# The order in which a ring of streamed weight tiles is filled, and when the last weights and weight sums are prepared, in a fused attention and two-MLP kernel

## The chip, the cores and the metric

One core of one Trainium2 chip runs the whole program. The metric is the device time of one execution in microseconds (us). TensorE (PE) does the matrix products and accumulates in PSUM; VectorE (DVE), ScalarE (ACT) and GpSimd (POOL) do the elementwise work; SyncE (SP) issues the transfers, each in program order: a transfer that waits holds back all that stands behind it in SP's queue.

## The reference

Attention in both directions between a sequence (512 rows) and a state (32 rows) for 8 batches and 8 heads, and then two MLPs on the 8 x 544 = 4352 rows that come out of it:

```python
x = np.ascontiguousarray(attn_out.transpose(0, 2, 1, 3)).reshape(B * S, H * D)

def _moe_ref(x, w_gate, w_val, w_out):      # d_model 512, d_ff 1536
    g = x @ w_gate
    silu = g * (1.0 / (1.0 + np.exp(-g)))
    return silu * (x @ w_val) @ w_out

def _moe2_ref(x, w_in, w_out):              # d_model 512, d_ff 2048
    h = x @ w_in
    g = h * (1.0 / (1.0 + np.exp(-1.702 * h)))
    return g @ w_out
```

All of the change lies in and around the second MLP, `_moe2_ref`.

## The kernel before, in words

Every fp32 operand of a product is kept as two tiles, a high part (a cast to `F32R`) and a low part (what the cast left over); a product is three matmuls: high by high, low by high, high by low. So each operand costs a cast on ACT and a subtraction on DVE (for activations, the helper `cut`, lines 720 to 722) or on POOL (for weights, lines 235 and 236).

Stage 1 (attention and the first MLP) runs block by block over the rows, and writes its result `y1` to DRAM. During its last block the weights of the second MLP are read and cut, in the order i2 0, o2 0, i2 1, o2 1, ... (`i2 f` is the f-th slice of `w_in`, `o2 f` that of `w_out`, F2 = 16 slices each). `need(key)` drives this: it runs `w_step` until that weight's cut has been recorded, and each step also asks for a later weight's transfer. At the end of stage 1 the slices up to 13 are done; i2 14, o2 14, i2 15 and o2 15 are not. The cut `o2` slices are also stored to DRAM as `w2b`, since their tiles in SBUF are wanted for other things.

Stage 2 (the loop at the end) goes over nine row blocks `n`: n = 0 is the block of the 256 state rows, n = 1 to 8 are the eight sequence blocks of 512 rows.

- n = 0 and n = 1: for each f, `mm_in` computes the hidden slice f (12 matmuls into one of the two `gv` buffers of PSUM), ACT takes a sigmoid, DVE multiplies (L1164), `to_h` cuts the result into a tile `h` and puts it into the list `waiting`. When more than two are waiting, `out2` takes the oldest and multiplies it with `o2 f` into the accumulators `acc0` to `acc3` (L330 to L332, three matmuls for each accumulator).
- n = 2 to 8: `four(n, p)` computes two hidden slices, 2p and 2p+1, at once, by Strassen's scheme: seven half-size products (42 matmuls of 256 columns, L1104 to L1106) of sums of weights with sums of activations. At its end it puts slice 2p+1 into `waiting` first and slice 2p second:

```python
        to_h(n, 2 * p + 1, sg, S)
        v.tensor_tensor(sf, one, sf, op=ALU.mult)
        to_h(n, 2 * p, sf, S)
```

  The two `out2` calls inside the next `four` consume them in that order. In the text such a `four` with its two `out2` is a pair.

From n = 1 on the `o2` slices no longer lie in SBUF; they are streamed back from `w2b` through a ring of three tiles `wo`. The list `stream2` says which slice is loaded next; `next_out` takes the next entry, puts it into ring place `s % 3` and issues one transfer of 512 KB on SP (L934). It is called three times at n = 0, f = 8, and then once at the end of each `out2`. A load into a ring place waits, on SP, until TensorE has used the tile that lies there.

The sums of weights that `four` needs are made during n = 0 and n = 1, for each of the PAIRS = 8 pairs of `i2` slices: `mix_load(p)` reads two `i2` slices back into a tile `sr` (two transfers, L960), `mix(p)` makes three sums on POOL (L974 to L976, in place in `sr`), casts them on ACT into tiles `wc` (L982) and takes the low parts on POOL (L983); `mix_store` writes full `wc` chunks to DRAM (`w2c`), from where `next_chunk` streams them again through another ring of three (L944) in n = 2 to 8. One more difference for each pair is made late, in n = 1 and just before n = 2 (`mix_late`, L989 to L992), from half slices (L958), and replaces a part of `i2`. `mix_step(n, f)` decides which of these run after step f: in the kernel before, a load in one step and all of `mix` in the next.

The other names that the rows use: `xr` are rows of `y1` read for the next block (L788, L1023), `xo` their cut parts, `ev` the copies of the accumulators on the way out (`evac`, L732 and L733), `sg` and `wt` working tiles.

Of the kernel before, what the change touches and what calls it, by code (L numbers as in the profile page):

```python
# [12 lines left out]
ALU = mybir.AluOpType  # L13
# [60 lines left out]
def kernel(  # L74
# [33 lines left out]
    F2 = FF2 // P  # L108
# [6 lines left out]
    v, a, pe, pool_e, sy = nc.vector, nc.scalar, nc.tensor, nc.gpsimd, nc.sync  # L115
# [19 lines left out]
    def f32(t):  # L135
        return t.bitcast(F32)
# [155 lines left out]
    def w_step(lead=2):  # L292
        w_join()
        if pos["begun"] > pos["done"]:
            w_end()
        w_dma()
        while pos["begun"] < len(stream):
            if pos["begun"] >= pos["done"] + (lead if stream[pos["begun"]][2] else 1):
                break
            w_begin()  # L300
            w_dma()

    def need(key):
        while pos["done"] <= where[key]:
            w_step()


    def mm_in(ps, w, xop, N, ks=range(KD)):

        for k in ks:  # L310
            xh, xl = xop[k]
            wh, wl = w[:, 0, k * P : (k + 1) * P], w[:, 1, k * P : (k + 1) * P]
            pe.matmul(ps[:, :N], wh, xh, start=k == 0, stop=False)  # L313
            pe.matmul(ps[:, :N], wl, xh, start=False, stop=False)  # L314
            pe.matmul(ps[:, :N], wh, xl, start=False, stop=k == KD - 1)  # L315
# [21 lines left out]
    def gv():  # L337
        return psg.tile([P, 512], F32, name="gv", tag="gv")
# [443 lines left out]
    def x2_step(n, f, at_f):  # L782

        N = NT if order2[n] == B else S
        for k in range(KD):
            if f == at_f + 2 * k:
                x2raw[k] = x2p.tile([P, 512], F32, name="xr", tag="xr", bufs=1)
                sy.dma_start(x2raw[k][:, :N], y1[order2[n]][k // 2][:, k % 2, :])  # L788
            if f == at_f + 2 * k + 2:
                xs2.setdefault(n, {})[k] = x_tiles(xp if n % 2 else x2q, k, N)  # L790
                cut(*xs2[n][k], x2raw.pop(k)[:, :N])

    order2 = [B] + list(range(B))
# [121 lines left out]
    Q = S // 2  # L915
    PAIRS = F2 // 2
# [5 lines left out]
    def slot(f, shape, name, dt=F32R):  # L922
        pl, tag = slot2[f]
        return pl.tile(shape, dt, name=name, tag=tag, bufs=1)

    stream2 = [(n, f) for n in range(1, len(order2)) for f in range(F2)]
    outs = {(0, f): units["o2", f] for f in range(F2) if ("o2", f) in units}
    pos2 = {"outs": 0, "chunks": 0}

    def next_out():  # L930
        s = pos2["outs"]
        if s < len(stream2):
            outs[stream2[s]] = t = slot(s % 3, [P, 2, DM], "wo")
            sy.dma_start(f32(t), both2[stream2[s][1]])  # L934
            pos2["outs"] += 1
# [3 lines left out]
    def next_chunk(load=True):  # L939
        c = pos2["chunks"]  # L940
        if c < NCH * (len(order2) - 1):
            mixed[c] = t = slot(3 + c % 3, [P, 2, 2, Q], "wc")
            if load:
                sy.dma_start(f32(t), chunks[c % NCH])  # L944
            pos2["chunks"] += 1

    def mixed_at(n, i):

        i += 3 * PAIRS * (n - 1)
        return mixed[i // 2][:, i % 2]  # L950

    sraw = {}

    def mix_load(p, late=False):
        sraw[p] = r = work.tile([P, 2, DM], F32, name="sr", tag="raw", bufs=RAWS)
        for j in range(2):
            if late:
                sy.dma_start(r[:, j, :Q], whole2["i2", 2 * p + j][:, :Q])  # L958
            else:
                sy.dma_start(r[:, j, :], whole2["i2", 2 * p + j])  # L960
# [3 lines left out]
    def mix_store():  # L964
        while full:
            c = full.pop(0)
            sy.dma_start(chunks[c], f32(mixed[c]))

    def mix(p):

        r = sraw.pop(p)
        a11, a12, a21, a22 = (r[:, j, c * Q : c * Q + Q] for j in range(2) for c in range(2))
        t = pool_e.tensor_tensor
        t(a22, a21, a22, op=ALU.add)  # L974
        t(a11, a22, a11, op=ALU.subtract)
        t(a12, a12, a11, op=ALU.subtract)  # L976
        for i, src in enumerate((a11, a22, a12)):
            k = 3 * p + i
            if k % 2 == 0:
                next_chunk(False)  # L980
            to = mixed_at(1, k)
            a.copy(to[:, 0], src)  # L982
            t(to[:, 1], src, f32(to[:, 0]), op=ALU.subtract)  # L983
            if k % 2 == 1:
                full.append(k // 2)

    def mix_late(p):
        r = sraw.pop(p)
        pool_e.tensor_tensor(r[:, 1, :Q], r[:, 0, :Q], r[:, 1, :Q], op=ALU.subtract)  # L989
        to = units["i2", 2 * p + 1][:, :, :Q]  # L990
        a.copy(to[:, 0], r[:, 1, :Q])
        pool_e.tensor_tensor(to[:, 1], r[:, 1, :Q], f32(to[:, 0]), op=ALU.subtract)  # L992

    def mix_step(n, f):

        mix_store()
        if n == 0 and f >= 7:
            if f % 2:
                mix_load((f - 7) // 2)
            else:  # L1000
                mix((f - 8) // 2)
        elif n == 1:
            if f in (0, 2, 4, 6):
                mix(4 + f // 2)
            if f in (1, 3, 5):
                mix_load(5 + f // 2)
            if f == 8:
                for _ in range(3):
                    next_chunk()
            if f >= 8:  # L1010
                if f > 8:
                    mix_late(f - 9)
                mix_load(f - 8, True)

    xs3 = {}
    xraw = {}
# [1 line left out]
    def x3_step(n, f):  # L1018

        if f == 1:  # L1020
            for j in range(2):
                xraw[j] = r = slot(XRAW[j], [P, 2, S], "xr", F32)
                sy.dma_start(r, y1[order2[n]][j])  # L1023
        if f < 3:
            return
        b11, b12 = xraw[0][:, :, :Q], xraw[0][:, :, Q:]
        b21, b22 = xraw[1][:, :, :Q], xraw[1][:, :, Q:]
        ops = {
            3: (0, b11),
            4: (b11, b12, b11),  # L1030
            5: (2, b22),
            6: (b12, b22, b12),
            7: (4, b11),
            8: (b11, b22, b11),
            9: (5, b11),
            10: (1, b21),
            11: (b21, b11, b21),
            12: (6, b12),
            13: (3, b21),
        }  # L1040
        op = ops.get(f)
        if op is None:
            return
        if len(op) == 3:
            v.tensor_tensor(op[0], op[1], op[2], op=ALU.subtract)
            return
        k, src = op
        if k < 4:
            t = (xp if n % 2 else x2q).tile([P, 2, 2, Q], F32R, name="xo", tag=f"x{k}")
        else:  # L1050
            t = slot(EXTRA[n % 2][k - 4], [P, 2, 2, Q], "xo")
        xs3.setdefault(n, {})[k] = t
        cut(t[:, 0], t[:, 1], src)
# [33 lines left out]
    def to_h(n, f, sg, N):  # L1087
        h = h_tile(count["h"] % 3)
        count["h"] += 1
        cut(h[:, 0, :N], h[:, 1, :N], sg[:, :N])  # L1090
        waiting.append((n, f, h))
# [51 lines left out]

    for n in range(len(order2)):
        N = NT if order2[n] == B else S
        if n == 2:
            mix_late(PAIRS - 1)
        for f in range(F2):
            if n > 1:
                if f % 2 == 0:  # L1150
                    four(n, f // 2)
                if n + 1 < len(order2):
                    x3_step(n + 1, f)
                continue
            if n == 0:
                need(("o2", min(f + 1, F2 - 1)))
                if f == 8:
                    for _ in range(3):
                        next_out()
            ps = gv()  # L1160
            mm_in(ps, units["i2", f], xs2[n], N)
            sg = work.tile([P, 512], F32, name="sg", tag="sg")
            a.activation(sg[:, :N], ps[:, :N], ACTF.Sigmoid, scale=1.702)
            v.tensor_tensor(sg[:, :N], ps[:, :N], sg[:, :N], op=ALU.mult)  # L1164
            to_h(n, f, sg, N)
            if n == 0:
                x2_step(1, f, 2)
            else:
                x3_step(2, f)
            mix_step(n, f)  # L1170
            if len(waiting) > 2:
                out2()
# [31 lines left out]
```

## Time and profile before

| what | us |
|---|---|
| time, median of 3 runs (lowest, highest) | 1657.43 (1656.83, 1658.67) |
| the profiled execution's own time | 1656.36 |
| its span (first to last instruction) | 1654.6 |
| TensorE matmul busy in the span | 1556.3 |
| VectorE, ScalarE, GpSimd busy | 911.7, 698.9, 377.3 |

Stage 1 takes the span up to some 835 us, n = 0 from there to 890, n = 1 to 983, n = 2 to 8 the rest. The page's slices show TensorE at 9 tenths nearly everywhere, and the transfers at 3 to 6 tenths of the engines' time. The clock granted to TensorE was 0.991 of full speed on the mean. A busy row of TensorE runs from a matmul's start to its modelled end, and matmuls overlap: so what a wait costs is read from the distance of two starts, against that distance where nothing waits.

### The profile page before, as it was taken

To read this page: it belongs to the slowest core of one execution; us is meant where nothing else is said; L and a number is where in the kernel's file an instruction comes from. 1 tells how busy PE (TensorE), PEld (TensorE's weight loads), DVE (VectorE), ACT (ScalarE), POOL (GpSimd) and SP (SyncE) were. 2 spreads that over 40 slices of the span, in tenths; PEclk is the share of its full clock that TensorE was granted. 3 is DMA by queue.
4 is the path that set the end of the run, shared out by engine and by line. 5 is a ranking of instruction groups with operands and counts; after the bars stand their busy time and mean duration, and the time that the engine had idled before them with its cause. 6 is when DMAs were issued, how large, how long until landed. Compare 5 with 4: busy or idle time off the path is not lost.

```text
span 1654.6 us, 21619 instructions
## 1 busy us (share of the span) xinstructions
PE 1556.3 (94%) x7960; PEld 1275.4 (77%) x7960; DVE 911.7 (55%) x1635; ACT 698.9 (42%) x1274; POOL 377.3 (23%) x314
## 2 busy tenths in 40 slices
PE   5999999999999999999996999999899989899997
PEld 2445778888888888898885888888788878788886
DVE  7673656858586777513332335555555555555543
ACT  5663556656464656434443332222222222222322
POOL 3332552424242333244525320000000000000000
PEclk9999999999999999999998999999999999999999
DMA  5662113425344343145655645363634545454443
GB/s 177 206 195 90 48 40 112 142 90 149 111 124 130 112 148 109 55 144 160 196 179 192 241 139 204 140 229 140 219 138 166 204 175 181 178 192 177 154 178 115
DMA packets 132130, 251.51 MB, mean 152 GB/s; under 512 B 49336, under 2 KB 60600, under 8 KB 132024
## 3 DMA queue, kind: packets, MB, share of 16 engines
q1 hardware_dynamic: 132024, 250.13, 45.3%
q8 instruction: 63, 1.03, 0.2%
q14 instruction: 43, 0.35, 0.1%
HBM read 205.52 MB, written 44.56 MB: 151 GB/s over the span
## 4 chain that ended last, share of the span: by engine, by line
PE 33%; DMA 14%; POOL 3%; issue 3%; ACT 0%; SPq 0%; DVE 0%; POOLq 0%; ACTq 0%
DMA wo<-w2b 12%; PE acc L330 8%; PE acc L332 7%; PE acc L331 7%; POOL wu L236 2%; PE gv L1106 2%; PE gv L1105 2%; PE gv L1104 2%; PE at L1104 1%; PE gv L313 1%; PE gv L314 1%; PE at L1105 1%; PE at L1106 1%; PE gv L315 1%; DMA sr<-w2i 1%
## 5 line engine op out<-in xcount | busy, mean ns | idle before, releaser
L330 PE MATMUL acc<-wo,h 128*128 128x512 f32 x512 | 205.5, 401 | 62.6 <-DMA wo<-w2b 58.5
L722 DVE TENSOR_TENSOR h<-sg,h 128x512 fp32r<-128x512 f32 (+1 forms) x240 | 175.7, 732 | 115.0 <-ACT h L721 112.8
L236 POOL TENSOR_TENSOR wu<-raw,wu 128x512 fp32r<-128x512 f32 x128 | 171.0, 1341 | 211.0 <-ACT wu L235 208.2
L721 ACT CAST h<-sg 128x512 fp32r<-128x512 f32 (+1 forms) x240 | 143.0, 596 | 151.7 <-DVE sg L1138 79.9
L331 PE MATMUL acc<-wo,h 128*128 128x512 f32 x512 | 201.3, 393 | 0.0
L332 PE MATMUL acc<-wo,h 128*128 128x512 f32 x512 | 201.3, 393 | 0.0
L1128 ACT ACTIVATE sg<-wt 128x512 f32<-128x512 f32 x56 | 35.4, 632 | 368.9 <-DVE wt L1126 368.9
L330 PEld LDWEIGHTS acc<-wo,h 128*128 128x128 f32 x512 | 96.7, 189 | 89.7 <-issue 59.9
L834 PE MATMUL acc<-h,wu 128*128 128x512 f32 (+1 forms) x384 | 148.5, 387 | 0.1
L835 PE MATMUL acc<-h,wu 128*128 128x512 f32 (+1 forms) x384 | 145.7, 380 | 1.5 <-POOL wu L236 1.5
L836 PE MATMUL acc<-h,wu 128*128 128x512 f32 (+1 forms) x384 | 145.7, 380 | 0.1
L320 PE MATMUL gv<-a,xo 128*128 128x512 f32 x336 | 137.6, 410 | 0.0
L1126 DVE TENSOR_TENSOR wt<-wt,gv 128x256 f32<-128x256 f32 x56 | 23.6, 421 | 205.5 <-PE gv L1106 205.5
L321 PE MATMUL gv<-a,xo 128*128 128x512 f32 x336 | 133.2, 396 | 0.0
L322 PE MATMUL gv<-a,xo 128*128 128x512 f32 x336 | 132.7, 395 | 0.0
L867 ACT ACTIVATE sg<-gv 128x512 f32<-128x512 f32 (+1 forms) x108 | 62.0, 574 | 134.5 <-PE gv L322 124.6
L332 PEld LDWEIGHTS acc<-wo,h 128*128 128x128 f32 x512 | 96.7, 189 | 21.3
L722 DVE TENSOR_TENSOR xo<-at,xo 128x512 fp32r<-128x512 f32 (+1 forms) x88 | 59.4, 675 | 95.3 <-ACT xo L721 94.8
L331 PEld LDWEIGHTS acc<-wo,h 128*128 128x128 f32 x512 | 96.9, 189 | 17.0
L880 DVE TENSOR_TENSOR sg<-gv,sg 128x512 f32<-128x512 f32 (+1 forms) x96 | 62.7, 653 | 66.3 <-PE gv L322 63.9
L1106 PE MATMUL gv<-xo,wu 128*128 128x256 f32 x336 | 95.6, 285 | 0.0
L1105 PE MATMUL gv<-xo,wu 128*128 128x256 f32 x336 | 95.1, 283 | 0.0
(177 smaller groups left out, 3675.5 us busy)
## 6 DMA issues: line engine op xcount, KB each, us to landing
wo<-w2b SPq DMA_DIRECT2D x128, 512.0 KB, 4.0
wc<-w2c SPq DMA_DIRECT2D x84, 512.0 KB, 5.8
raw<-w1o SPq DMA_DIRECT2D x96, 256.0 KB, 2.8
raw<-in_moe_w_out_dram SPq DMA_DIRECT2D x28, 512.0 KB, 4.2
y<-ev SPq DMA_DIRECT2D x16, 512.0 KB, 2.8
raw<-in_moe_w_in_dram SPq DMA_DIRECT2D x16, 512.0 KB
w2b<-wu SPq DMA_DIRECT2D x16, 512.0 KB, 3.4
out_dram<-ev SPq DMA_DIRECT2D x16, 512.0 KB, 7.7
```

What stands on the lines that cost most here:

```text
L236: pool_e.tensor_tensor(u[:, 1, :], t, f32(u[:, 0, :]), op=ALU.subtract)
L320: pe.matmul(ps, wh, xh, start=k == 0, stop=False)
L330: pe.matmul(ps, lh, rh, start=first, stop=False)
L331: pe.matmul(ps, lh, rl, start=False, stop=False)
L332: pe.matmul(ps, ll, rh, start=False, stop=last)
L721: a.copy(h_, src)
L722: v.tensor_tensor(l_, src, f32(h_), op=ALU.subtract)
L834: pe.matmul(ps, w[:, 0, c], h[:, 0, :N], start=f == 0, stop=False)
L835: pe.matmul(ps, w[:, 1, c], h[:, 0, :N], start=False, stop=False)
L836: pe.matmul(ps, w[:, 0, c], h[:, 1, :N], start=False, stop=f == F1 - 1)
L1105: pe.matmul(ps, w[:, 1, c], x_[:, 0, kt], start=False, stop=False)
L1106: pe.matmul(ps, w[:, 0, c], x_[:, 1, kt], start=False, stop=kt == 1)
```

## The change

Three edits, all in stage 2:

1. `stream2` lists the slices from n = 2 on as `f ^ 1`, that is 1, 0, 3, 2, ..., instead of 0, 1, 2, 3, ...; the list for n = 1 stays 0 to 15.
2. In n = 0, `need(("o2", min(f + 1, F2 - 1)))` in each step becomes `need` of i2 14, o2 14, i2 15 and o2 15 in the steps f = 2, 3, 4 and 5.
3. `mix` and `mix_late` are each cut into two functions, `mix_add` and `mix_cut`, `late_add` and `late_cut`; `mix_step` counts the steps of n = 0 and n = 1 through (`s = n * F2 + f`) and runs, for pair p, the load in step 6 + 2p (before: 7 + 2p), the sums in step 7 + 2p (before: 8 + 2p) and the cut in step 8 + 2p (as before). For the late differences: load in step 24 + p (as before), difference in 25 + p (as before), cut in 26 + p (before: 25 + p); so the last ones fall into the first two steps of n = 2, where `mix_step` is now called.

```diff
-    stream2 = [(n, f) for n in range(1, len(order2)) for f in range(F2)]
+    stream2 = [(n, f if n == 1 else f ^ 1) for n in range(1, len(order2)) for f in range(F2)]
...
+    def mix_add(p):
+
+        a11, a12, a21, a22 = quarters(p)
         t = pool_e.tensor_tensor
         t(a22, a21, a22, op=ALU.add)
         t(a11, a22, a11, op=ALU.subtract)
         t(a12, a12, a11, op=ALU.subtract)
+
+    def mix_cut(p):
+        a11, a12, _, a22 = quarters(p)
         for i, src in enumerate((a11, a22, a12)):
...
     def mix_step(n, f):
 
         mix_store()
-        if n == 0 and f >= 7:
-            if f % 2:
-                mix_load((f - 7) // 2)
-            else:
-                mix((f - 8) // 2)
...
+        s = n * F2 + f
+        for back, fn in ((2, mix_cut), (1, mix_add), (0, mix_load)):
+            p, odd = divmod(s - back - 6, 2)
+            if not odd and 0 <= p < PAIRS:
+                fn(p)
...
+        for back, fn in ((2, late_cut), (1, late_add), (0, lambda p: mix_load(p, True))):
+            p = s - back - F2 - 8
+            if 0 <= p < PAIRS:
+                fn(p)
...
             if n > 1:
+                if n == 2:
+                    mix_step(n, f)
                 if f % 2 == 0:
                     four(n, f // 2)
...
             if n == 0:
-                need(("o2", min(f + 1, F2 - 1)))
+                if 1 < f < 6:
+                    need(("io"[f % 2] + "2", F2 - 3 + f // 2))
```

The first place is in n = 2. On SP, before, the loads stand in this order (`w2b3_152` is slice 3, and the tile that it fills is `wo_8628`; `wc` are the weight sums):

```order
L934 DMA wo_8628<-w2b3_152 128x1024
L934 DMA wo_8670<-w2b4_153 128x1024
L944 DMA wc_8679<-w2c4_7301 128x1024
L944 DMA wc_8681<-w2c5_7302 128x1024
L934 DMA wo_8731<-w2b5_154 128x1024
L934 DMA wo_8773<-w2b6_155 128x1024
```

On TensorE, before, the first matmul of five successive `out2` (the tile is the first operand after the arrow):

```order
L330 MATMUL acc0_8612<-wo_8628,h_8672 128x512
...
L330 MATMUL acc0_8612<-wo_8556,h_8676 128x512
...
L330 MATMUL acc0_8612<-wo_8731,h_8775 128x512
...
L330 MATMUL acc0_8612<-wo_8670,h_8779 128x512
...
L330 MATMUL acc0_8612<-wo_8833,h_8877 128x512
```

The tiles are used in another order than that in which they are filled. The same place with the change, on SP:

```order
L934 DMA wo_8628<-w2b2_151 128x1024
L934 DMA wo_8670<-w2b5_154 128x1024
L944 DMA wc_8679<-w2c4_7301 128x1024
L944 DMA wc_8681<-w2c5_7302 128x1024
L934 DMA wo_8731<-w2b4_153 128x1024
L934 DMA wo_8773<-w2b7_156 128x1024
```

and on TensorE, five successive `out2` again:

```order
L330 MATMUL acc0_8610<-wo_8554,h_8672 128x512
...
L330 MATMUL acc0_8610<-wo_8628,h_8676 128x512
...
L330 MATMUL acc0_8610<-wo_8670,h_8775 128x512
...
L330 MATMUL acc0_8610<-wo_8731,h_8779 128x512
...
L330 MATMUL acc0_8610<-wo_8773,h_8877 128x512
```

Filling and use now go in the same order, and the loads of `wc` stand where they stood.

The second place is ACT in the last steps of n = 0 (f = 12 to 14; L1163 is the sigmoid, L721 the cut of `h`, L235 the cast of an `i2` or `o2` slice, L982 that of the weight sums). Before:

```order
L982 CAST wc<-sr 128x256 x3
L235 CAST wu<-raw 128x512 x2
L1163 ACTIVATE sg<-gv 128x256
L721 CAST h<-sg 128x256
L235 CAST wu<-raw 128x512 x2
```

With the change, from the cast of the weight sums of the same pair on (lines are renumbered, L1163 is L1169, L982 is L987):

```order
L987 CAST wc<-sr 128x256 x3
L1169 ACTIVATE sg<-gv 128x256
L721 CAST h<-sg 128x256
L1169 ACTIVATE sg<-gv 128x256
L721 CAST h<-sg 128x256
```

The four L235 casts are gone from here; they stand in the steps f = 2 to 5, one ahead of each sigmoid.

The third place is SP at the start of n = 0 (`raw` takes an uncut slice, `w2b_163` and `w2b_164` are the stores of o2 14 and o2 15, `xr` rows of the next block, `sr` the first load for the weight sums):

```order
 L905 DMA y_7_2_7295<-ev 128x1024
-L788 DMA xr<-y_0_0_998 128x512 x2
+L181 DMA raw<-w2i_147 128x512
+L788 DMA xr<-y_0_0_998 128x512
+L240 DMA w2b_163<-wu 128x1024
+L181 DMA raw<-w2o_148 128x512
+L788 DMA xr<-y_0_0_998 128x512
+L240 DMA w2b_164<-wu 128x1024
 L788 DMA xr<-y_0_2_1003 128x512
 L960 DMA sr<-w2i_117 128x512
```

Two loads and two stores move from the end of n = 0 to its start, ahead of and between the loads of `xr`.

## Rows read from the trace of the kernel before

**Rows 1.** The page, chain that ended last, shares by line

```profile
DMA wo<-w2b 12%; PE acc L330 8%; PE acc L332 7%; PE acc L331 7%; POOL wu L236 2%; PE gv L1106 2%; PE gv L1105 2%; PE gv L1104 2%; PE at L1104 1%; PE gv L313 1%; PE gv L314 1%; PE at L1105 1%; PE at L1106 1%; PE gv L315 1%; DMA sr<-w2i 1%
```

**Rows 2.** Windows: length, then busy of PE, PEld, DVE, ACT, POOL, PEclk, DMA

```profile
100.00:760.00 660.00, 657.36 (x3043) 520.50 (x3042) 413.91 (x700) 363.76 (x654) 240.00 (x179) 1.00 0.36 108
830.00:906.00 76.00, 62.44 (x348) 54.12 (x347) 22.50 (x44) 28.71 (x66) 30.49 (x37) 0.93 0.53 189
998.00:1650.00 652.00, 593.31 (x3623) 527.63 (x3621) 342.78 (x682) 182.79 (x330) 0.00 (x0) 1.00 0.48 174
```

**Rows 3.** Waits from 998 us on: total us, times, longest us

```profile
PE acc L330 <- DMA wo<-w2b: 58.5, 55, 3.4
```

**Rows 4.** Timeline of PE, one pair: start, length, instruction, idle time before and releaser

```profile
1331.61 0.40 PE L330 MATMUL acc<-wo,h 128*128 128x512 f32 x1
...
1334.36 0.28 PE L1104 MATMUL gv<-xo,wu 128*128 128x256 f32 x1
...
1337.11 0.28 PE L1106 MATMUL at<-xo,wu 128*128 128x256 f32 x1
1338.72 0.47 PE L330 MATMUL acc<-wo,h 128*128 128x512 f32 x1 [1.33 <-DMA wo<-w2b]
...
1341.55 0.28 PE L1104 MATMUL gv<-xo,wu 128*128 128x256 f32 x1
```

**Rows 5.** Timeline of SP in the same pair

```profile
1334.55 0.79 SPq L934 DMA_DIRECT2D wo<-w2b  x2
1335.39 0.90 SPq L944 DMA_DIRECT2D wc<-w2c  x2
```

**Rows 6.** All transfers of `wo`, issue to landing

```profile
DMA to landing us min/median/max: 3.2/4.0/6.7
```

**Rows 7.** All transfers of `wc`, issue to landing

```profile
DMA to landing us min/median/max: 2.9/5.7/7.6
```

**Rows 8.** Timeline of DVE in the same pair, the low part of the next `h`

```profile
1333.65 0.69 DVE L722 TENSOR_TENSOR h<-sg,h 128x512 fp32r<-128x512 f32 x1 [0.69 <-ACT h L721]
```

**Rows 9.** Timeline of PE at the end of n = 0 and the start of n = 1

```profile
869.62 0.39 PE L332 MATMUL acc<-wu,h 128*128 128x512 f32 x1
872.02 0.39 PE L313 MATMUL gv<-xo,wu 128*128 128x256 f32 x1 [2.01 <-DVE sg L1164]
...
874.70 0.39 PE L332 MATMUL acc<-wu,h 128*128 128x512 f32 x1
880.60 0.58 PE L313 MATMUL gv<-xo,wu 128*128 128x256 f32 x1 [5.50 <-ACT wu L235]
882.92 0.58 PE L314 MATMUL gv<-xo,wu 128*128 128x256 f32 x1 [1.74 <-POOL wu L236]
...
887.99 0.41 PE L313 MATMUL gv<-xo,wu 128*128 128x256 f32 x1
...
901.71 0.39 PE L315 MATMUL gv<-xo,wu 128*128 128x512 f32 x1
906.17 0.79 PE L330 MATMUL acc<-wo,h 128*128 128x512 f32 x1 [4.07 <-ACT ev L732]
...
911.45 0.63 PE L313 MATMUL gv<-xo,wu 128*128 128x512 f32 x1
```

**Rows 10.** Timeline of ACT there, the casts of the weight sums

```profile
870.01 1.21 ACT L982 CAST wc<-sr 128x256 fp32r<-128x256 f32 x3 [3.92 <-POOL sr L975]
...
878.81 1.21 ACT L982 CAST wc<-sr 128x256 fp32r<-128x256 f32 x3 [4.91 <-POOL sr L975]
...
902.55 1.21 ACT L982 CAST wc<-sr 128x256 fp32r<-128x256 f32 x3 [5.48 <-POOL sr L975]
```

**Rows 11.** Timeline of POOL there

```profile
859.56 1.02 POOL L974 TENSOR_TENSOR sr<-sr 128x256 f32<-128x256 f32 x1 [23.63 <-DMA sr<-w2i]
...
868.43 0.73 POOL L974 TENSOR_TENSOR sr<-sr 128x256 f32<-128x256 f32 x1 [4.12 <-DMA sr<-w2i]
...
870.74 2.10 POOL L983 TENSOR_TENSOR wc<-sr,wc 128x256 fp32r<-128x256 f32 x3
```

**Rows 12.** Timeline of SP there

```profile
864.00 1.31 SPq L960 DMA_DIRECT2D sr<-w2i  x2
```

More of the change, by code (lines that the diff above doesn't have):

```diff
@@ L967, in mix_store, with quarters @@
             sy.dma_start(chunks[c], f32(mixed[c]))
-    def mix(p):
-        r = sraw.pop(p)
-        a11, a12, a21, a22 = (r[:, j, c * Q : c * Q + Q] for j in range(2) for c in range(2))
+    def quarters(p):
+        return [sraw[p][:, j, c * Q : c * Q + Q] for j in range(2) for c in range(2)]
+    def mix_add(p):
+        a11, a12, a21, a22 = quarters(p)
         t = pool_e.tensor_tensor
@@ L982, in mix, with late_add, late_cut @@
             a.copy(to[:, 0], src)
-            t(to[:, 1], src, f32(to[:, 0]), op=ALU.subtract)
+            pool_e.tensor_tensor(to[:, 1], src, f32(to[:, 0]), op=ALU.subtract)
             if k % 2 == 1:
                 full.append(k // 2)
-    def mix_late(p):
-        r = sraw.pop(p)
-        pool_e.tensor_tensor(r[:, 1, :Q], r[:, 0, :Q], r[:, 1, :Q], op=ALU.subtract)
+        del sraw[p]
+    def late_add(p):
+        a11, _, a21, _ = quarters(p)
+        pool_e.tensor_tensor(a21, a11, a21, op=ALU.subtract)
+    def late_cut(p):
+        src = quarters(p)[2]
         to = units["i2", 2 * p + 1][:, :, :Q]
-        a.copy(to[:, 0], r[:, 1, :Q])
-        pool_e.tensor_tensor(to[:, 1], r[:, 1, :Q], f32(to[:, 0]), op=ALU.subtract)
+        a.copy(to[:, 0], src)
+        pool_e.tensor_tensor(to[:, 1], src, f32(to[:, 0]), op=ALU.subtract)
+        del sraw[p]
     def mix_step(n, f):
         mix_store()
-        if n == 0 and f >= 7:
-            if f % 2:
-                mix_load((f - 7) // 2)
-            else:
-                mix((f - 8) // 2)
[L1002 to L1013, printed above, removed]
+        s = n * F2 + f
[3 more added lines that the diff above has]
+                fn(p)
+        if s == F2 + 8:
+            for _ in range(3):
+                next_chunk()
+        for back, fn in ((2, late_cut), (1, late_add), (0, lambda p: mix_load(p, True))):
+            p = s - back - F2 - 8
+            if 0 <= p < PAIRS:
+                fn(p)
     xs3 = {}
@@ L1145 @@
         N = NT if order2[n] == B else S
-        if n == 2:
-            mix_late(PAIRS - 1)
         for f in range(F2):
             if n > 1:
+                if n == 2:
+                    mix_step(n, f)
                 if f % 2 == 0:
```

## The prediction

> **What bounds the kernel now.** I read the chain that ended last first. Its largest entry is a transfer: loads of `wo` hold 12% of the span [rows 1], more than any line of TensorE. Next the busy time by stage. TensorE matmuls fill 657.4 of 660 us in the middle of stage 1, but 593 of 652 us in n = 2 to 8, and 62.4 of 76 us in the stretch that holds n = 0; DVE, ACT and POOL are half idle or more in both [rows 2]. So TensorE is the bound everywhere, and what can be won is where it stands still: some 59 us in n = 2 to 8 and 14 us around n = 0.
>
> In n = 2 to 8 the waits give one answer: L330, the first matmul of an `out2`, waits for `wo` 55 times, 58.5 us together [rows 3]. 55 is once a pair, not once an `out2`. The timeline of one pair shows which: the `out2` at 1331.61 starts without a wait, the one at 1338.72 after 1.33 us [rows 4]. SP shows why: both loads of the pair are issued together at 1334.55, just when the `out2` that began at 1331.61 is done [rows 5]. The first of them fills the place of slice 2p, which is used second, so it waits on SP for the second use and holds the other load back; the tile that it fills, slice 2p+3, is wanted first in the next pair, 2.9 us of products later (1334.36 to 1337.11, and 0.12 for the last) [rows 4]. It lands 4 us after its issue [rows 6]. The wait is the difference.
>
> Around n = 0, TensorE stops four times [rows 9]: at 872.02 for DVE's L1164, which stands behind ACT's casts of the weight sums at 870.01, which waited 3.92 us for POOL [rows 10]; at 880.60 and 882.92 for the cast and low part of i2 14, asked for only in step 13 and again behind such casts (878.81, a wait of 4.91 us) [rows 9, 10]; at 906.17 for the copy of an accumulator, behind the casts of 902.55 and their 5.48 us [rows 9, 10]. POOL in turn waited for the load: issued at 864.00, used at 868.43 [rows 11, 12]. Load, sums and casts in two neighbouring steps are a chain longer than a step. After two of these stops the matmuls run at half speed for some us.
>
> **Edit 1, the order of the ring: -71.7 us.** A stalled start costs more than the idle time that the view counts. From 1337.11 to 1338.72 are 1.61 us; two such matmuls in a row start 0.12 us apart ((1337.11 - 1334.36) / 23). So the loss is 1.49, which is 0.16 over the 1.33 shown; and the stalled `out2` takes 1341.55 - 1338.72 = 2.83 us where the unstalled one takes 1334.36 - 1331.61 = 2.75, 0.08 more [rows 4]. 55 waits with 58.5 us, and 55 x 0.24 = 13.2 us beside them, an estimate from this one pair: 71.7 us. No instruction and no byte is added.
>
> What is late next? With the change a load is issued at the end of the use of its place's old tile, and its tile is used three `out2` later: in between are two `out2` (5.5 us) and three stretches of products (18 + 24 + 18 of them, 7.2 us), 12.7 us in all, against a longest landing of 6.7 us [rows 6]. So the ring is no longer near the edge. The next operand of that `out2`, `h`, is complete at 1333.65 + 0.69 = 1334.34 [rows 8], 2.9 us ahead of the 1337.23 at which TensorE would want it; it hangs on products that TensorE made earlier, so the lead stays when the wait goes. Third are the `wc` loads, which stand behind the `wo` loads on SP; they are a rival below. So I take the whole 71.7, and a pair of 10.5 us instead of some 11.8.
>
> **Edits 2 and 3, the last units and the weight sums: -19.6 us.** The four stops, again from start to start (0.12 us a matmul of 256 columns, 2.75 / 12 = 0.23 one of 512) [rows 4, 9]: 869.62 to 872.02 less 0.23 is 2.17; 874.70 to 880.60 less 0.23 is 5.67; 880.60 to 882.92 less 0.12 is 2.20; 901.71 to 906.17 less 0.23 is 4.23. The slow matmuls: 882.92 to 887.99 holds 11 of 256 and 6 of 512 columns, 5.07 us instead of 2.70, 2.4 lost; 906.17 to 911.45 holds 12 of 512 columns, 5.28 instead of 2.75, 2.5 lost, and some 0.4 in the first matmuls after the two stretches. Sum 19.6 us. Both stretches stand behind the stops of 5.50 and 4.07 us and nowhere else, so they go with these.
>
> What the edits put in their place. A step of n = 0 is 12 x 0.12 + 6 x 0.23 = 2.8 us of TensorE. The four units now cost ACT one cast each in the steps 2 to 5, and POOL one low part each: the same instructions as before. SP takes two loads of `raw` and two stores more there, past which the loads of `xr` move; each waits for POOL's low part. The load of i2 15 can go only when the tile of i2 14 is cut, so it lands about when step 4 wants it (two steps, 5.6 us, for a cast, a low part and a load of some 4 us): ACT may stand up to 1 us there. TensorE has two `gv` buffers and works on `out2` in between, so a sigmoid may be late by about one step before it shows; I cost this at nothing, and at 1 us if that cover is gone. The first weight sums gain little: their load stands behind an `xr` load on SP. From the second on the load goes out at the end of one step, POOL sums in the next and ACT casts in the one after; POOL's three sums (3 x 0.73) and three low parts (2.10) are 4.3 us for two steps of 5.6 [rows 11], so POOL keeps up and ACT finds its sums ready. The copy of the accumulator at 906.17 then stands behind no cast that waits. The late differences are cast a step later, under the 5.4 us steps of n = 1, and the last under the first pair of n = 2: nothing.
>
> **The sum.** Span 1654.6 - 71.7 - 19.6 = 1563.3. Around the span lie 1656.4 - 1654.6 = 1.8 us, and the median of the runs is 1.1 over the profiled execution: 1566 us.
>
> **Rivals.**
>
> A. POOL stays last around n = 0. For it: the sum at 859.56 took 1.02 us, the one at 868.43 took 0.73 [rows 11]; six instructions at 1.02 are 6.1 us, more than two steps, and then the casts wait again and the stops at 872 and 906 stay (2.17, 4.23, 2.5 and some 0.3 us). Only i2 14 is won. Time 1566 + 9.2 = 1575. Against: one row of the three is long, and a step of slack lies before TensorE. The Trainium skill, "SBUF — State Buffer", section "Who interferes with whom", states that a DVE instruction with two SBUF inputs, as every low part of `h` is, contends with a GpSimd instruction that reads SBUF; by that rule long POOL rows are to be expected and the time is this rival's 1575; the trace agrees in part, with 1.02 against 0.73.
>
> B. The `wc` loads become the late ones. After every second pair two chunks are asked for, and the first is wanted by the last product of the very next pair: 24 products, one `out2` and 12 products on, 2.9 + 2.75 + 1.4 = 7.1 us after SP sees the end of the `out2`. One `wo` issue stands ahead of it, about 0.6 us. So 6.5 us are left for a landing of 5.7 in the median and 7.6 at most [rows 7]. At 7.6 each time, 1.1 us x 28 pairs = 31 us come back: 1597. Against: today two `wo` are issued ahead of it [rows 5], with the change one, the other 5 us earlier; so it shares the engines with less.
>
> C. The order doesn't fit, and each pair goes on waiting: then only the 19.6 us are won, 1638. The listing of the order speaks against it.
>
> D. Slower than before, by the clock: when TensorE no longer pauses, its granted clock falls in n = 2 to 8. At half speed an `out2` of 12 matmuls takes 5.28 us instead of 2.75 [rows 4, 9], nearly twice. The 91.3 us won are spent when some 99 us of the 590 us of products (56 pairs x 10.5) run so: from a sixth of the stage on it is slower than before, and at a fifth it is about 1675. Against it: the 660 us of stage 1 have TensorE busy to 657 us at a granted clock of 1.00 [rows 2], so full work has not lowered it here; half speed is seen only after stops.
>
> **How the numbers follow.** Forecast 0.74, within 1559 to 1572 (the 1 us of step 4, and some us for what the start-to-start reckoning of one pair leaves open); A 0.11, B 0.09 (from nothing to 31 us), C 0.03, D 0.03. The likeliest gives 1566. The range reaches over A and the near part of B, 1559 to 1584, and leaves out the rest of B, C and D and what I have not thought of, under 0.2. Faster by over 0.2% (about 3 us, what a measurement of this kernel can tell from no change) are forecast, A, B and C; slower D; the same hardly anything: 0.96, 0.01, 0.03.
>
> **What would show it.** Right: no L330 of n = 2 to 8 waits for `wo`; in SP's timeline the two `wo` of a pair stand about 5 us apart; pairs are 10.5 us long; TensorE is busy over 98% of n = 2 to 8; between the start of n = 0 and 900 us no stop over 1 us, and the granted clock there is 1.00. Edit 1 wrong: a new releaser stands before L330 (`h` from DVE) or before L1104 (`wc`). Edits 2 and 3 wrong: casts of weight sums still wait for POOL by several us, or a cast of i2 15 for its load, with TensorE's matmuls behind them.

## The result, and the profile after

The changed kernel takes 1564.63 us (median of 4 runs, 1564.0 to 1565.0), the kernel before 1657.13 (4 runs, 1655.27 to 1658.67): a ratio of 0.9442, 95% interval 0.9426 to 0.9458, 5.6% less. The forecast was 1566 us, 1.4 us more; faster was given 0.96. The profiled execution's span is 1563.1 us, against 1563.3 in the sum; most of the 1.4 us is the 1.1 that the sum adds for the median over the profiled execution, where this time the median is 0.2 under it.

The chain that ended last, by line (it answers to [rows 1]):

```profile
PE acc L331 8%; PE acc L330 8%; PE acc L332 8%; PE gv L1111 3%; PE gv L1110 3%; PE gv L1109 3%; PE at L1109 3%; PE at L1110 3%; PE at L1111 3%; PE gv L313 1%; PE gv L315 1%; PE gv L314 1%; DMA sr<-w2i 0%; POOL sr L976 0%; POOL sr L977 0%
```

The loads of `wo` are gone from it; what is left is TensorE's own work (lines are renumbered: L1104 to L1106 are now L1109 to L1111, L974 to L976 are L976 to L978, L982 is L987, L1163 is L1169). The stages, with the columns of [rows 2]:

```profile
100.00:760.00 660.00, 657.37 (x3045) 520.77 (x3044) 413.89 (x700) 364.38 (x654) 239.87 (x178) 1.00 0.36 108
830.00:906.00 76.00, 74.91 (x418) 64.98 (x417) 29.80 (x53) 34.81 (x79) 40.89 (x49) 1.00 0.72 251
906.00:998.00 92.00, 92.00 (x477) 79.05 (x476) 40.69 (x69) 30.63 (x59) 18.72 (x23) 1.00 0.57 196
998.00:1560.00 562.00, 560.71 (x3499) 506.83 (x3498) 332.42 (x661) 176.48 (x318) 0.00 (x0) 1.00 0.55 193
```

Stage 1 is as it was. TensorE is busy for 560.7 of 562 us in the last row, and for 74.9 of 76 where it had 62.4, and the granted clock is 1.00 in all four. The waits of TensorE from 840 us to the end, all of them:

```profile
PE gv L313 <- DVE sg L1170: 0.7, 1, 0.7
```

Against [rows 3] and the four stops of [rows 9] one wait of 0.7 us is left. (A wait of 0.4 us in the third step of n = 0 lies just ahead of this window and is in both kernels, at 838.76 us before and at 838.20 after.) In n = 2 to 8 there is none. One pair on TensorE, from the second `out2` of one pair over the 24 products that follow it to the first `out2` of the next (it answers to [rows 4]):

```profile
1318.53 0.28 PE L1111 MATMUL at<-xo,wc 128*128 128x256 f32 x1
1318.64 0.39 PE L330 MATMUL acc<-wo,h 128*128 128x512 f32 x1
...
1324.16 0.28 PE L1111 MATMUL at<-xo,wu 128*128 128x256 f32 x1
1324.28 0.40 PE L330 MATMUL acc<-wo,h 128*128 128x512 f32 x1
...
1326.80 0.39 PE L332 MATMUL acc<-wo,h 128*128 128x512 f32 x1
1327.03 0.28 PE L1109 MATMUL gv<-xo,wu 128*128 128x256 f32 x1
```

The `out2` at 1324.28 is the one that used to wait; it starts 0.12 us after the matmul before it and takes 2.75 us. And SP there (it answers to [rows 5]; a merged row of x2 runs from the first issue to the end of the second):

```profile
1321.60 0.32 SPq L934 DMA_DIRECT2D wo<-w2b  x1
1321.97 1.25 SPq L944 DMA_DIRECT2D wc<-w2c  x2
1327.22 5.25 SPq L934 DMA_DIRECT2D wo<-w2b  x2
1332.52 0.42 SPq L944 DMA_DIRECT2D wc<-w2c  x1
1337.77 5.25 SPq L934 DMA_DIRECT2D wo<-w2b  x2
```

The two `wo` of a pair are issued 5 us apart, each at the end of its own `out2`, and only one of them stands just ahead of the `wc` loads.

Where the time came from, by the timeline of TensorE (from the first matmul of a stage to the first of the next; for n = 2 to 8 to the last matmul's start):

| stage | before, us | after, us | less |
|---|---|---|---|
| n = 0 | 55.65 | 44.12 | 11.53 |
| n = 1 | 91.76 | 84.52 | 7.24 |
| n = 2 to 8 | 667.10 | 594.91 | 72.19 |

### The profile page after: what moved, and what is told of

Same layout as the page of the kernel before. It is cut to its first block, busy times and chain, and to the rows that moved or that the text cites. A ratio compares the mean times of both kernels' runs of the same rounds, so it can differ in the third digit from the quotient of the medians.

```text
span 1563.1 us, 21672 instructions
## 1 busy us (share of the span) xinstructions
PE 1536.8 (98%) x7960; PEld 1268.0 (81%) x7960; DVE 912.8 (58%) x1635; ACT 699.0 (45%) x1274; POOL 379.0 (24%) x314
## 5 line engine op out<-in xcount | busy, mean ns | idle before, releaser
L721 ACT CAST h<-sg 128x512 fp32r<-128x512 f32 (+1 forms) x240 | 143.0, 596 | 152.3 <-DVE sg L1143 80.2
L331 PE MATMUL acc<-wo,h 128*128 128x512 f32 x512 | 200.7, 392 | 0.0
L330 PE MATMUL acc<-wo,h 128*128 128x512 f32 x512 | 200.2, 391 | 0.0
L332 PE MATMUL acc<-wo,h 128*128 128x512 f32 x512 | 199.8, 390 | 0.0
L332 PEld LDWEIGHTS acc<-wo,h 128*128 128x128 f32 x512 | 96.1, 188 | 20.9
L220 POOL TENSOR_TENSOR wt<-wt,raw 128x512 uint32<-128x512 uint32 x44 | 57.7, 1311 | 157.5 <-DVE wt L217 60.7
L1111 PE MATMUL gv<-xo,wu 128*128 128x256 f32 x336 | 95.6, 285 | 0.0
```

Source lines behind the costliest of these rows:

```text
L330: pe.matmul(ps, lh, rh, start=first, stop=False)
L331: pe.matmul(ps, lh, rl, start=False, stop=False)
L332: pe.matmul(ps, ll, rh, start=False, stop=last)
L721: a.copy(h_, src)
L1111: pe.matmul(ps, w[:, 0, c], x_[:, 1, kt], start=False, stop=kt == 1)
```

## The experiments

The experiments ran on two chips. The kernel before, run beside them, takes 1640.7 to 1642.6 us there, some 15 less than in the first runs, whose chip is not known; so each ratio below is against the runs of before on the same chip, and where an expectation gives a time worked out from 1657 us, it is the gain that can be compared. What the 15 us are is the last group's question. The stages of all runs, read as in the table above:

| run | n = 0 | n = 1 | n = 2 to 8 | median time |
|---|---|---|---|---|
| order only (edit 1) | 55.67 | 91.88 | 594.88 | 1586.24 |
| units only (edit 2) | 48.74 | 93.25 | 649.53 | 1634.47 |
| sums only (edit 3) | 50.07 | 84.62 | 651.16 | 1628.81 |
| units and sums (2 and 3) | 43.44 | 84.52 | 650.92 | 1621.69 |
| ring of two | 43.11 | 84.52 | 597.23 | 1566.65 |
| ring of one | 43.04 | 104.95 | 766.59 | 1755.38 |
| ring of four, old order | 43.84 | 84.92 | 610.27 | 1576.93 |
| the same, sums first | 43.35 | 84.93 | 596.01 | 1567.99 |
| ring filled later | 43.03 | 85.69 | 594.91 | 1564.97 (one run) |
| before again | 56.71 | 91.75 | 650.18 | 1639.81 (one run) |
| after again | 43.50 | 84.52 | 594.88 | 1565.72 |

### Each edit alone

**Edit 1 alone**: the kernel before with the new line of `stream2`.

> The kernel before with edit 1 alone (the loads of n = 2 to 8 in the order 1, 0, 3, 2, ...). Theory: the wait of one out2 a pair is all that the order costs, 71.7 us by start-to-start distances, and it does not hang on the other edits: 1657 - 72 = 1585 us, n = 2 to 8 at 595 us from the first L1104 to the last matmul as with all three edits, no wait of L330 for wo, and the four stops around n = 0 as before (2.0, 5.5, 1.7 and 4.1 us idle). Rival: the stops around n = 0 shift work into n = 2, and a part of the gain shows only with all three edits: above 1590 us.

Measured: 1586.24 us, ratio 0.9651 (0.9635 to 0.9666). All waits of TensorE from 840 us on:

```profile
PE gv L313 <- ACT wu L235: 5.5, 1, 5.5
PE acc L330 <- ACT ev L732: 4.2, 1, 4.2
PE gv L313 <- DVE sg L1164: 3.0, 3, 2.2
PE gv L314 <- POOL wu L236: 1.7, 1, 1.7
```

The stops around n = 0 stand as before, none for `wo` is left, and n = 2 to 8 takes 594.88 us, within 0.03 us of the run with all edits. So edit 1 does its work alone. The time of 1585 was met; the gain of 72 us was not, since the kernel before is 15 us faster here: 56 us. What edit 1 is worth hangs on how long the kernel before waits; the time that it leads to does not.

**Edit 2 alone**: the kernel before with the new `need`.

> The kernel before with edit 2 alone (the last four units asked for in steps 2 to 5; sums and casts still in one step). Theory: the stop of 5.5 and 1.7 us for i2 14 goes, but the chain of load, sums and casts still takes some 8.7 us for two steps of 5.6, so that ACT's casts hold TensorE in the steps 12 and 14 and at the copy of the accumulator: a gain of 4 to 9 us, 1648 to 1653 us, with stops behind casts of weight sums still there. Rival: the units were the whole of it and the sums harmless: 1657 - 18 = 1639 us.

Measured: 1634.47 us, ratio 0.9952 (0.9936 to 0.9969), 8 us less by the medians (forecast 4 to 9), 5.4 by the stages n = 0 and n = 1. TensorE's stops at the end of n = 0 and at the accumulator, from its timeline:

```profile
872.13 0.49 PE L313 MATMUL gv<-xo,wu 128*128 128x256 f32 x1 [2.05 <-DVE sg L1165]
...
881.08 0.38 PE L313 MATMUL gv<-xo,wu 128*128 128x256 f32 x1 [1.50 <-DVE sg L1165]
...
889.39 0.50 PE L313 MATMUL gv<-xo,wu 128*128 128x512 f32 x1 [1.15 <-DVE sg L1165]
...
901.13 0.80 PE L330 MATMUL acc<-wo,h 128*128 128x512 f32 x1 [4.56 <-ACT ev L732]
```

and the casts of weight sums that ACT stood in (the last two):

```profile
887.37 1.22 ACT L982 CAST wc<-sr 128x256 fp32r<-128x256 f32 x3 [4.40 <-POOL sr L975]
...
897.51 1.21 ACT L982 CAST wc<-sr 128x256 fp32r<-128x256 f32 x3 [5.76 <-POOL sr L975]
```

The stop for i2 14 is gone, but each pair of weight sums still holds ACT for 4 to 6 us, and TensorE now stops there instead. The rival, that the units were all of it, falls.

**Edit 3 alone**: the changed kernel with the old line of `stream2` and the old `need`.

> The kernel before with edit 3 alone (weight sums in three steps; the last four units asked for in steps 13 and 14). Theory: the stops at 872 and 906 us go (2.2 and 4.2 us, and 2.5 us of half speed), the casts wait for POOL by under 3 us; in step 14 or 15 TensorE still stops for i2 14 or i2 15, by 3 to 7 us: a gain of 8 to 14 us, 1643 to 1649 us. Rival: the units are harmless once ACT is free, 1639 us.

Measured: 1628.81 us, ratio 0.9919 (0.9898 to 0.9941), 14 us less (forecast 8 to 14), 12.7 by the stages. TensorE's stops in its timeline:

```profile
870.04 0.39 PE L313 MATMUL gv<-xo,wu 128*128 128x256 f32 x1 [0.82 <-DVE sg L1169]
...
874.45 0.38 PE L313 MATMUL gv<-xo,wu 128*128 128x256 f32 x1 [1.35 <-ACT wu L235]
876.77 0.39 PE L314 MATMUL gv<-xo,wu 128*128 128x256 f32 x1 [1.93 <-POOL wu L236]
...
881.73 0.38 PE L314 MATMUL gv<-xo,wu 128*128 128x256 f32 x1 [0.35 <-POOL wu L236]
```

The stop at the accumulator is gone and n = 1 has its 84.6 us; what stays are 3.6 us for i2 14 and i2 15, and 0.82 us at 870.04. So edit 3 cures the larger part, and shrinks even the stop that edit 2 is for, since ACT stands behind POOL for 0.8 us just ahead of the cast of i2 14, where before it was 4.91 [rows 10].

**Edits 2 and 3 without 1**: the changed kernel with the old line of `stream2`.

> The changed kernel with the loads of the ring in the old order 0, 1, 2, 3, ... (edits 2 and 3 without 1). Theory: the terms add up, so the gain is that of n = 0 and n = 1 alone, 18 to 19 us: 1638 to 1640 us, L330 waits 55 times for wo, 58 us together. Rival: without edit 1 a part of what is won around n = 0 is lost again at the waits of the first pairs: over 1643 us.

Measured: 1621.69 us, ratio 0.9866 (0.985 to 0.9882), 20.9 us less; n = 0 and n = 1 together 127.96 us, 19.4 less than in the first profile of before (forecast 18 to 19). Its wait in n = 2 to 8:

```profile
PE acc L330 <- DMA wo<-w2b: 38.0, 52, 3.4
```

The gain around n = 0 is near the forecast whether edit 1 is there or not. The waits for `wo` are nearly as many as forecast, 52 and three more, 1.7 us together, that the view puts down to ACT, but shorter: 0.73 us each, where [rows 3] have 1.06.

### What the order of the ring buys

**Two places.** In the changed kernel:

```diff
-            outs[stream2[s]] = t = slot(s % 3, [P, 2, DM], "wo")
+            outs[stream2[s]] = t = slot(s % 2, [P, 2, DM], "wo")
...
-                    for _ in range(3):
+                    for _ in range(2):
```

> The changed kernel with two places in the ring instead of three (two loads at the start, place s % 2). Theory: what counts is the stretch between the end of a tile's use and the use of the tile that takes its place. With two places in the order of use that is one out2 and two stretches of products, 2.75 + 2.2 + 2.9 = 7.8 us in n = 2 to 8 and one out2 and two products of 2.75 us in n = 1, against a median landing of 3.7 and a longest of 5.8 us: no wait, 1565 us, the same as with three places. Rival: the number of places is what the order bought, and two places bring a wait of about a microsecond a pair back: 1620 us or more.

Measured: 1566.65 us (1562.5 to 1567.9), ratio 0.9546 (0.9526 to 0.9566); the changed kernel itself has 0.9538 (0.9522 to 0.9554, the last run below), so the two can't be told apart. The waits for `wo`:

```profile
PE acc L330 <- DMA wo<-w2b: 1.2, 2, 0.7
```

Two waits in the 112 `out2` of n = 2 to 8. One is in the last `out2` of the program, where no product stands ahead of it. The other, at 1155.32 us, is near the start of a block: its load was issued at 1147.09, behind two stores of `out` and two loads of `xr`, and took some 8 us, longer than the 5.8 that the expectation reckoned with. With the right order two places do what three did not do with the wrong one, so three places were not too few in themselves.

**One place**: `slot(0, ...)`, and a single `next_out()` at the start.

> The changed kernel with a single place. Theory: the stretch is then one stretch of products, 2.16 or 2.88 us in turn, and 2.75 us in n = 1, against some 3.8 us from the end of an out2 to the landing: waits of about 1.7 and 1.0 us and 0.1 us for each restart, 2.8 us a pair for 56 pairs and 1.1 us for 16 steps of n = 1, together some 170 us: 1735 us, between 1710 and 1760. Rival: a load that has the engines to itself lands so fast that it hides behind the products: below 1650 us.

Measured: 1755.38 us, ratio 1.0706 (1.0683 to 1.0729). A pair and the start of a block on SP, and the waits of TensorE there:

```profile
1300.84 6.66 SPq L934 DMA_DIRECT2D wo<-w2b  x2
1307.55 0.90 SPq L944 DMA_DIRECT2D wc<-w2c  x2
1313.77 6.67 SPq L934 DMA_DIRECT2D wo<-w2b  x2
1320.53 1.47 SPq L1088 DMA_DIRECT2D out_dram<-ev  x2
1322.05 0.89 SPq L944 DMA_DIRECT2D wc<-w2c  x1
1322.99 2.14 SPq L1028 DMA_DIRECT2D xr<-y  x2
1326.95 0.32 SPq L934 DMA_DIRECT2D wo<-w2b  x1
```

```profile
1304.14 0.47 PE L330 MATMUL acc<-wo,h 128*128 128x512 f32 x1 [1.20 <-ACT sg L1138]
...
1310.75 0.47 PE L330 MATMUL acc<-wo,h 128*128 128x512 f32 x1 [0.73 <-DMA wo<-w2b]
...
1333.46 0.77 PE L330 MATMUL acc<-wo,h 128*128 128x512 f32 x1 [4.39 <-ACT xo L721]
```

(Two of these waits are put down to ACT instructions; but the matmuls start 3.3 and 6.5 us after the issues of `wo` at 1300.84 and 1326.95, and so are taken as waits for those.) The stretch rule holds: nearly every `out2` waits now. The time is 20 us over the 1735 forecast, and within the range given. A pair inside a block costs near what was reckoned (from 1304.14 to 1317.10 are 12.96 us, 2.5 over 10.5, where 2.8 were reckoned); what I left out are the starts of blocks, where, by the order on SP, the load of `wo` shares the engines with stores of `out` and loads of `xr`, and TensorE waits 3.3 to 4.5 us, six times, and twice at the end, where no products stand ahead; these eight waits are some 18 us over the mean of 1.5 that I had reckoned for them. At the start of the last block, which has the stores but no `xr` to load, the wait is 1.2 us. And I left out the clock, which falls to half after each of the eight, here after the one that ends at 1115.86:

```profile
1115.00:1121.00 6.00, 5.14 (x12) 4.11 (x13) 1.99 (x4) 1.14 (x2) 0.00 (x0) 0.50 0.02 5
```

The `out2` behind such a wait takes 4.1 to 5.3 us instead of 2.8, which is 11.6 us more for the six alone. What keeps the sum at 20 us is that the pairs inside the blocks cost less than reckoned.

**Four places with the old order**: `stream2` of the kernel before in the changed kernel, and

```diff
-            outs[stream2[s]] = t = slot(s % 3, [P, 2, DM], "wo")
+            outs[stream2[s]] = t = slot((0, 1, 2, 15)[s % 4], [P, 2, DM], "wo")
...
+            if (n, f) == (1, 2):
+                next_out()
             ps = gv()
```

> The changed kernel with the loads in the old order 0, 1, 2, 3, ... but four places in the ring (the fourth is the tile of o2 15, first filled at n = 1, f = 2). Theory: the order hurt because a load for the place of a tile that is used second held back the load of the tile that is used first in the next pair; with a fourth place that tile is there already, a whole pair ahead, and no L330 waits for wo. But both wo loads of a pair are issued together again, ahead of the two wc loads, whose first has only some 6.2 us left: a few tenths of a us may come back there. 1565 to 1572 us. Rival 1: a wait once a pair remains, 1635 us. Rival 2 (the wc loads are next to be late): L1104 waits for wc by over half a us in most second pairs, 1580 us or more.

Measured: 1576.93 us (1572.7 to 1582.9), ratio 0.9604 (0.9578 to 0.9631), 11 us over the changed kernel. TensorE waits for `wo` nowhere, and in n = 2 to 8 for this alone:

```profile
PE at L1109 <- DMA wc<-w2c: 8.8, 13, 1.2
```

So a fourth place does away with the wait that the order makes, as the theory has it; but then rival B of the prediction comes true, smaller than its 31 us: the profiled execution, the slowest of the four, takes 15.4 us more in n = 2 to 8. Both `wo` loads of a pair again stand ahead of the `wc` loads, in a pair that is now 1.3 us shorter. My range for it, up to 1572, was too low; rival 2's half a microsecond came in 8 of the 28 second pairs.

**The same with the sums first**: the two `next_out` of a pair moved behind its `next_chunk`.

```diff
         for i in range(3 * p + 3 * PAIRS * (n - 1), 3 * p + 3 + 3 * PAIRS * (n - 1)):
             if i % 2 == 1:
                 next_chunk()
+        next_out()
+        next_out()
```

> The run with four places and the old order again (e6_ring_four_natural), but in n = 2 to 8 the two wo loads of a pair are issued at its end behind the wc loads instead of ahead of them. Theory: the 8.8 us of waits for wc in e6 come from the two wo loads that stood ahead on the same queue, not from a third thing such as more traffic; with wc first they land in about 4 us and no L1104 waits; the wo loads have a whole pair, so n = 2 to 8 takes 595 us again and the run 1565 us (1563 to 1568). Rival: the wc loads are late because all transfers of a pair stand together, whatever their order; then a wait for wc or wo stays, 1572 us or more.

Measured: 1567.99 us (1565.7 to 1568.3), ratio 0.9551 (0.9536 to 0.9565); no wait of TensorE is left from 840 us on, and n = 2 to 8 takes 596.0 us. With the same transfers in another order on the queue the waits for `wc` are gone, so it was the `wo` loads ahead of them. The landing of `wc` in the run before this one and in this one, from issue:

```profile
DMA to landing us min/median/max: 4.3/6.9/9.1
```

```profile
DMA to landing us min/median/max: 3.7/4.9/8.8
```

The median fell by 2 us, but not to the forecast 4.

### The stop that is left

```diff
-                if f == 8:
+                if f == 12:
                     for _ in range(3):
                         next_out()
```

> The changed kernel with the first three loads of the ring at n = 0, f = 12 instead of f = 8. Theory: the one stop over half a us that is left around n = 0, 0.7 us of idle time at 870.33 us, comes from the second load of weight sums, which took 6.3 us to be used because three wo loads and an xr load stand ahead of it; with the wo loads moved away POOL starts the second sums 1 to 2 us earlier and the stop is gone: 1 us less, 1563 to 1565 us, too little to be told from no change by the time, but plain in the timeline. Rival: the stop comes from the first sums, whose load stands behind xr, and stays.

Measured: one run, 1564.97 us. In the changed kernel POOL starts the second sums late, at 866.19, behind their load:

```profile
866.19 1.28 POOL L976 TENSOR_TENSOR sr<-sr 128x256 f32<-128x256 f32 x1 [1.61 <-DMA sr<-w2i]
```

In this run:

```profile
864.21 0.74 POOL L976 TENSOR_TENSOR sr<-sr 128x256 f32<-128x256 f32 x1 [0.36 <-DMA sr<-w2i]
```

The stop at 870 is gone, n = 0 is 1.1 us shorter, and n = 1 is 1.2 us longer: the three loads now stand ahead of other loads of weight sums, and a stop of 0.87 us comes at 882.94. Ahead of it the cast of weight sums waits 5.74 us for POOL, and POOL for its load:

```profile
879.33 0.74 POOL L976 TENSOR_TENSOR sr<-sr 128x256 f32<-128x256 f32 x1 [5.50 <-DMA sr<-w2i]
```

Nothing is won: the stop moves with those loads, which bears the theory out. That the stop at 870 is gone would not show it by itself: with the loads where they were it is 0.70 us in the changed kernel, 0.19 in its second profile, 0.56 in the ring of four and nothing in the ring of four with the sums first. But POOL starts the second sums 31.1 to 31.7 us after the first matmul of n = 0 in these four, and after 29.4 us here.

### Why the kernel before is faster in the later runs

The kernel before, unchanged, with a profile; and the changed kernel, unchanged, with runs beside it.

> The kernel before, unchanged, profiled on the chip of this call. On the chips of the experiments it took 1642 us where the profiled one took 1657. Theory: the difference lies in n = 2 to 8 alone and is the landing of the wo loads, 3.3 us in the median for the first of a pair instead of 3.7, for 55 pairs: n = 2 to 8 takes some 650 us instead of 667, n = 0 and n = 1 the same 55.7 and 91.8. Rival: the difference is spread over the whole kernel (another clock): stage 1 is shorter too.

> The changed kernel, unchanged, on the chip of this call. Theory: since no load is waited for, its time does not hang on how fast they land: 1564 to 1566 us as on the first chip, while the kernel before is at 1642: a ratio of 0.953 instead of 0.944. Rival: the changed kernel is faster on this chip as well, by the same 15 us, 1550 us.

Measured: before 1639.81 us (one run; 1640.66 in the median of seven more on this chip), after 1565.72 us (1564.65 to 1566.81), ratio 0.9538 (0.9522 to 0.9554). Stage 1 of the kernel before in this run, as in the first of [rows 2], and its wait for `wo`:

```profile
100.00:760.00 660.00, 657.37 (x3049) 520.42 (x3048) 415.09 (x701) 365.25 (x657) 241.18 (x179) 1.00 0.36 109
```

```profile
PE acc L330 <- DMA wo<-w2b: 40.9, 53, 3.4
```

n = 2 to 8 takes 650.2 us instead of 667.1; n = 1 is as long as in the first profile and n = 0 is 1.1 us longer. The first `wo` of a pair lands 3.34 us after its issue here (median of the 16 for which the trace has it), 3.69 in the first profile (of 15). A wait is 0.77 us on the mean instead of 1.06. So the time of the kernel before hangs on how fast a load lands, 55 times over, and that of the changed one does not: its n = 2 to 8 takes 594.88 us here and 594.91 in the first profile.

## Why the prediction was right, point by point

- **The bound, and which `out2` waits: right.** Edit 1 alone removes all waits for `wo` and leaves the stops around n = 0, and with two places the right order has two short waits in place of 55. The mechanism, a load that waits on SP for the second use and holds back the tile that is used first, is shown from a second side by the ring of four, where the old order has no wait for `wo`.
- **Edit 1, 71.7 us: measured 72.2** between the first two profiles (667.10 to 594.91). The start-to-start reckoning was needed: the view's 58.5 us of idle time alone would have fallen 13.7 us short. That one pair stood for 55 did no harm: by the distances of starts, all the waits of n = 2 to 8 in the trace of before lose 0.16 us beyond their idle time on the mean, as that pair did. Its other reading, that DVE is half idle or more in n = 2 to 8, is a little off (343 of 652 us busy); nothing hung on it.
- **Edits 2 and 3, 19.6 us: measured 18.8** (11.53 and 7.24). Most of the missing 0.8 us is the stop at 870.33; in the second profile of the changed kernel, where that stop is 0.19 us, the two stages are 19.4 us shorter. I had said that the first sums gain little, and had costed that at nothing; it was the second sums, behind the `wo` and `xr` loads, that were late by 1.6 us, and a part of it reached TensorE. The half speed after the two stops went with them, as put: the granted clock is 1.00 in all four rows above, where the stretch of n = 0 had 0.93 [rows 2]. That the two misses, 0.5 us more and 0.8 us less, all but cancel in the sum is luck.
- **What was costed at nothing.** ACT stood at the cast of i2 15 for 0.28 us and at that of o2 15 for 0.24, under the 1 us allowed, and TensorE did not notice:

```profile
844.37 0.62 ACT L235 CAST wu<-raw 128x512 fp32r<-128x512 f32 x1 [0.28 <-DMA raw<-w2i]
...
847.68 0.62 ACT L235 CAST wu<-raw 128x512 fp32r<-128x512 f32 x1 [0.24 <-DMA raw<-w2o]
```

- **Rival A, POOL last around n = 0: not so.** The casts of weight sums in the changed kernel wait for POOL 3.0 us at the first pair, 2.2 at the second and then 0.7; the third on ACT:

```profile
872.89 0.71 ACT L987 CAST wc<-sr 128x256 fp32r<-128x256 f32 x2 [0.67 <-POOL sr L977]
```

  POOL's rows do get longer beside DVE: the 1.28 us row at 866.19 above runs with the low part of a cut of `xo` on DVE from 866.18 on, where 0.74 is usual. The Trainium skill, "SBUF — State Buffer", section "Who interferes with whom", states that a DVE instruction with two SBUF inputs, as that one is, contends with a GpSimd instruction that reads SBUF; the trace agrees. But mostly one or two of the six rows of a pair get longer, and from the third pair on POOL's six follow each other in 4.7 us, against two steps of 5.6. The slack is thin: after the late second load POOL works without a pause from 866.2 to 883.0 us before it has caught up.
- **Rival B, the `wc` loads: did not come, but is the next in line.** No L1109 waits in the changed kernel. With both `wo` loads ahead of them, as in the ring of four, thirteen do, and with none ahead again none. So the reason given against it, that only one `wo` stands ahead now, holds.
- **Rival C and D: no.** No pair waits, and the granted clock in n = 2 to 8 is 1.00 with TensorE busy for 99.8% of it.

By stage times against the first profile, edit 2 alone wins 5.4 us, edit 3 alone 12.7 and both 19.4. The two add up to 1.3 us less than both together, but the kernel before differs by 1.0 us in these stages between its own two profiles, so no interplay of the two edits is shown. The prediction had put them into one sum, and nothing in it hung on that.

## What to carry to other kernels

Fill a ring in the order in which it is emptied: a load that must wait for a tile used later holds back, in an in-order queue, the load of the tile needed next. Three places did not help against that here; a fourth did, but put the next loads in the queue late until they were issued first. The stretch between the end of one use and the next use of that place, against the longest landing, told beforehand where the rings of three, two and one would wait, all but at the starts of blocks, where other transfers stand ahead and a load takes longer. Price a stall from start to start, not by its idle time: here each of 55 cost 0.25 us more than the view showed (72.2 us less 58.5). A kernel with exposed loads carries their landing time in its own, and that made 15 us between the first runs and the later ones here, more than many changes are worth: compare such kernels side by side.

## What the runs showed of the hardware that I had not expected

The same load of 512 KB lands in 3.69 us in one profile of the same kernel and in 3.34 in another (medians of the first `wo` of a pair), and the kernel, which waits for it 55 times, differs by 15 to 17 us, while TensorE's busy time in 660 us of stage 1 is the same to 0.01 us. Whether the chip makes the difference or where the tensors lie in its memory was not tried. And transfers that are issued together land one after the other: of the two `wo` of a pair in the kernel before the second landed after 4.95 us in the median (of 13, between 4.25 and 6.65), with 0.4 us between the issues.

I had not looked for half speed in the run with a single place either: after each of the eight waits of 3.3 to 4.5 us TensorE ran at a granted clock of 0.50 for some us, while between 1300 and 1317 us, with waits of 1.20, 0.73 and 1.21 us, it stayed at 1.00.
